# The second mixture's second round: two lists in two quarters each, in place of four lists in one quarter each

## The chip, the cores and the metric

The kernel runs on one core of one Trainium2 chip. The time is the device time of one execution in microseconds (us); three executions of the kernel before gave 761.75, 761.96 and 762.65 us, median 761.96 us.

## The reference

Three layers run one after the other on 2304 tokens of width 512, in float32: windowed attention, a dense feed-forward layer, and a mixture of eight experts of which each token uses the one with the highest logit. The change is in the mixture:

```python
expert_idx = np.argmax(logits, axis=1)
gate_w = probs[np.arange(N), expert_idx]
for e in range(E):                       # E = 8 experts, D = 512, F = 1024
    mask = expert_idx == e
    h = np.maximum(x[mask] @ w1[e], 0.0)      # [n, 512] @ [512, 1024]
    out[mask] = gate_w[mask, None] * (h @ w2[e])   # [n, 1024] @ [1024, 512]
```

How many tokens an expert gets is known only when the logits are there.

## The kernel before, in words

The kernel picks the expert that most tokens chose and computes it for all 17 tiles of 128 tokens; rows of other experts' tokens are not written out. This dense expert is the loop over `e_up` and `e_down`: 40 slots (5 blocks of 4, 4, 4, 3 and 2 tiles, 8 slots each). In slot q TensorE does `e_up(q)`, 12 matmuls into `eh` over 512, 384 or 256 columns by the size of the block, and `e_down(q - 2)`, three matmuls of 512 columns into `eo` for each tile. Both read operands that were split into a high and a low part.

The tokens of the other seven experts are put in lists of 32 rows, one expert to a list. Four lists make a step (class `Quad`): their 128 rows are gathered into one tile `yg`, transposed (`qt`, into `yTh`), multiplied with w1 in two halves of 512 columns, relu'd into `hb`, transposed again into `hTh` and multiplied with w2. All lists have different weights, so list i uses the 32 columns of the array that write rows 32i to 32i+31 of `qo` (line 1227): four matmuls of 32 rows x 512 columns stand one after the other, in plain float32, and each leaves two records in the trace. Such a step has 16 substeps of four matmuls; each substep takes four pieces of weights of 256 KB, in pairs in eight buffers `rw` of 512 KB.

Nothing is scheduled: the order of each engine is the order in which the code is written (`manual_schedule`). `second()` puts extra work behind slots of the dense expert as hooks. Two rounds are put there, `quads[0]` and `quads[1]`: substeps n and n+1 (counted over both rounds) are computed behind slot 15 + 3n/4 and their loads are issued from SP's queue three slots earlier. SP waits there in order until TensorE has read the buffers. The loads of the second round carry a condition (is there such a list?); a list that isn't there is issued and moves nothing. Lists beyond the eight of the two rounds are done behind a branch at the end (line 1476), which is taken when the number of lists is over 8.

Behind the last substep `put` scales the 128 rows with their gates on VectorE (line 1167) and writes them to their tokens' places with an indirect DMA from GpSimd's queue (line 1168).

Of the kernel before, what the change touches and what calls it, by code (L numbers as in the profile page):

```python
# [9 lines left out]
F32 = mybir.dt.float32  # L10
F32R = mybir.dt.float32r
BF16 = mybir.dt.bfloat16
U32 = mybir.dt.uint32
I32 = mybir.dt.int32
AF = mybir.ActivationFunctionType
ALU = mybir.AluOpType
# [7 lines left out]
    trans=[10.354, 10.896, 16.524, 22.659], pglob=[9.223, 14.082, 14.125, 22.293],  # L24
# [12 lines left out]
def kernel(  # L37
# [16 lines left out]
    nc = tc.nc  # L54
    B, H, S, D = q_l.shape
    G = q_g.shape[2]
    P = 128
    DM = H * D
# [4 lines left out]
    KD = DM // P  # L63
    KF = DFF // P
    KF2 = F2 // P
    NTOK = B * S + B * G
    NTILE = B * NT + 1
    QW = 32
    NQ4 = P // QW
    NSTEP = -(-(NTOK // QW + E) // NQ4)  # L70
# [16 lines left out]
        out=tri_bf, in_=ones_bf, pattern=[[1, P]], compare_op=ALU.is_gt, fill=0.0, base=0, channel_multiplier=-1  # L87
# [3 lines left out]
    bigs = const.tile([P, NSTEP], F32, name="bigs")  # L91
    nc.gpsimd.iota(
        bigs, pattern=[[P, NSTEP]], base=2 * NTOK, channel_multiplier=1, allow_small_or_imprecise_dtypes=True
# [22 lines left out]
    NC = 8  # L116
# [9 lines left out]
    ps = at_st.enter_context(tc.tile_pool(name="ps", bufs=3, space=PSUM))  # L126
# [10 lines left out]
    for c in range(2):  # L137
        rows = mask[c * HP : (c + 1) * HP]
        nc.gpsimd.affine_select(
            out=rows[:, :, :HP], in_=rows[:, :, :HP], pattern=[[0, 3], [1, HP]], compare_op=ALU.is_ge, fill=NEG,  # L140
# [184 lines left out]
    class Unit:  # L325
        def __init__(self, n):
            self.b, self.g = divmod(n, 2)
            self.kw = [None, None]
            self.qT = [None, None]
            self.sm = {}  # L330
            self.sg = {}
            self.pn = {}
            self.xs = {}
            self.st = {}
            self.pt = {}
            self.ptA = {}
# [188 lines left out]
    def trans(n, k):  # L525
        u = units[n]
        hl, uu = divmod(k, 2)
        pn = u.pn.pop(k)
        ta = ps.tile([P, 4, P], F32, name="ta", tag="T")
        tb = ps.tile([P, 512], F32, name="tb", tag="T")  # L530
        ptA = get_ptA(n, k)
        ptB = ap_.tile([P, P], F32, name="ptB", tag="ptB")
        u.pt[k] = ptA, ptB
        for i in range(4):
            nc.tensor.transpose(ta[:, i, :], pn[:, i, :], ident)  # L535
        nc.tensor.transpose(tb[:, :P], u.sg.pop(k).rearrange("p i g -> p (i g)"), ident)
        copy(AT["e_ta"], ptA[:, :, G:], ta)
        copy(AT["e_tb"], ptB, tb[:, :P])
# [385 lines left out]

    NS1 = 2
    R = {}

    def pick():  # L930
# [75 lines left out]
    def norms(t0, t1):  # L1006
        sl = slice(t0, t1)
        nc.gpsimd.tensor_tensor(
            out=gt[:, 0, sl], in0=ssq[:, sl], in1=half.to_broadcast([P, t1 - t0]), op=ALU.pow
        )  # L1010
# [117 lines left out]
    outs = dram_disjoint_views(out, NTILE + NSTEP)  # L1128
    w1r = w1.rearrange("e (k p) f -> e k p f", p=P)
    w2r = w2.rearrange("e (k i p) d -> e k p i d", p=P, i=2)  # L1130
    raws = [None] * NC
# [32 lines left out]
    def put(j, ops):  # L1164
        ids = R["ids"]
        ob = rp.tile([P, DM], F32, name="ob", tag="ob0")
        nc.vector.tensor_scalar(out=ob, in0=ops, scalar1=R["gsl"][:, j : j + 1], scalar2=None, op0=ALU.mult)
        nc.gpsimd.indirect_dma_start(
            out=outs[NTILE + j], out_offset=bass.IndirectOffsetOnAxis(ap=ids[:, j : j + 1], axis=0), in_=ob, in_offset=None,
            bounds_check=NTOK - 1, oob_is_err=False,  # L1170
        )
# [4 lines left out]
    class Quad:  # L1176
# [7 lines left out]
        def regs(self, i0, i1):  # L1184
            exi = R["exi"]
            for i in range(i0, i1):
                q = NQ4 * self.j + i
                ev = nc.sync.value_load(exi[0:1, 0, q : q + 1], min_val=0, max_val=E - 1)
                ch = nc.sync.value_load(exi[0:1, 1, q : q + 1], min_val=0, max_val=1) if self.j else None
                self.e.append((ev, {"cond": ch} if self.j else {}))  # L1190
# [15 lines left out]
        def load(self, s):  # L1206
            n = NSUB * self.j + s
            for p in range(2):
                t = self.raw[s, p] = raws[(2 * n + p) % NC].rearrange("p (i d) -> p i d", i=2)
                for i in range(2):  # L1210
                    ev, kw = self.e[2 * p + i]
                    if s < 2 * KD:
                        f, k = divmod(s, KD)
                        src = w1r[bass.ds(ev, 1), k, :, f * 512 : (f + 1) * 512]
                    else:
                        src = w2q[bass.ds(ev, 1), s - 2 * KD]
                    nc.sync.dma_start(out=t[:, i, :], in_=src.rearrange("e p f -> (e p) f"), **kw)

        def mm(self, s):
            first, last = (s % KD == 0, s % KD == KD - 1) if s < 2 * KD else (s == 2 * KD, s == NSUB - 1)  # L1220
            if first:
                self.o = ps.tile([P, 512], F32, name="qo", tag="T")
            a, c = (self.yT, s % KD) if s < 2 * KD else (self.hT, s - 2 * KD)
            ws = [self.raw.pop((s, p)) for p in range(2)]
            for i in range(NQ4):
                cs = slice(QW * i, QW * (i + 1))
                nc.tensor.matmul(self.o[cs], lhsT=a[:, c, cs], rhs=ws[i // 2][:, i % 2, :], start=first, stop=last)
            if last and s < 2 * KD:
                self.hb = rp.tile([P, 512], F32, name="hb")
                nc.scalar.activation(out=self.hb, in_=self.o, func=AF.Relu)  # L1230

        def htr(self, f):
            self.tr(self.hb, self.hT[:, 4 * f : 4 * f + 4, :])
# [2 lines left out]
            put(self.j, self.o)  # L1236


    NES = NEB * KF2
    eb = [Blk() for _ in range(NEB)]  # L1240
    eq = {}
# [70 lines left out]
    def hook(q, *fs):  # L1312
        hooks.setdefault(q, []).extend(fs)

    def second():

        for c in range(6, NC):
            hook(c - 6, lambda c=c: es_split(c))
        for b in range(1, NEB):
            q, nt = KF2 * (b - 1), eblocks[b][1]  # L1320
            if b > 1:
                hook(q + 1, lambda b=b: e_load(b, 0), lambda b=b: e_load(b, 1))
                q += 3
            for i in range(nt):
                hook(q + i, lambda b=b, i=i: e_tr(b, i))
                if i + 2 < nt:
                    hook(q + i, lambda b=b, i=i: e_load(b, i + 2))
        TE = blocks[NB - 2][0] // P
        hook(-11, lambda: norms(0, TE))
        hook(-7, lambda: gates(0, TE))  # L1330
        hook(-5, lambda: members(0, TE))
        hook(8, steps_e)
        hook(9, steps_e2, lambda: members(TE, NTILE), steps1b)
        hook(10, steps1c, lambda: quads[0].regs(0, NQ4))
        hook(11, steps2, lambda: norms(TE, NTILE))
        quads = [Quad(j) for j in range(NS1)]
        hook(12, quads[0].gather)
        hook(13, lambda: gates(TE, NTILE))
        hook(14, quads[0].trans)
        hook(14, lambda: R.update(rl=digits(R["ohhi"], NTILE, NSTEP, gb)))  # L1340
        hook(15, lambda: R.update(gsl=gate_list(R["rl"])))
        hook(26, lambda: R.update(nst=nc.values_load(R["exi"][0:1, 0, NQ:], min_val=0, max_val=NQ)))
        for n in range(0, NS1 * NSUB, 2):
            (j, s), q = divmod(n, NSUB), 15 + 3 * n // 4
            r = quads[j]
            hook(q - 3, lambda r=r, s=s: (r.load(s), r.load(s + 1)))
            hook(q, lambda r=r, s=s: (r.mm(s), r.mm(s + 1)))
            if s in (KD, 2 * KD):
                hook(q, lambda r=r, s=s: r.htr(s // KD - 1))
            if s == KD and j + 1 < NS1:  # L1350
                hook(q, lambda j=j: quads[j + 1].regs(0, NQ4))
            if s == 2 * KD and j + 1 < NS1:
                hook(q, lambda j=j: quads[j + 1].gather())
            if s == NSUB - 4 and j + 1 < NS1:
                hook(q, lambda j=j: quads[j + 1].trans())
            if s == NSUB - 2:
                hook(q, lambda r=r: r.put())

    cvq = [(i, h) for i in range(ncv) for h in range(2)]
    rp = None  # L1360
# [6 lines left out]
    with tc.manual_schedule():  # L1367
# [105 lines left out]
        for i in range(eblocks[NEB - 1][1]):  # L1473
            e_down(NES - 2, [i])
            e_down(NES - 1, [i])
    with tc.If(R["nst"] > NS1 * NQ4):  # L1476
        with tc.manual_schedule():
            for j in range(NS1, NSTEP):
                r = Quad(j)
                r.regs(0, NQ4)  # L1480
                r.gather()
                r.trans()
                for s in range(3):
                    r.load(s)
                for s in range(NSUB):
                    if s + 3 < NSUB:
                        r.load(s + 3)
                    r.mm(s)
                    if s in (KD - 1, 2 * KD - 1):
                        r.htr(s // KD)  # L1490
                r.put()
# [30 lines left out]
```

## Time and profile before

| | |
|---|---|
| device time, three executions | 761.75 / 761.96 / 762.65 us |
| the profiled execution | 760.9 us |
| its span, first to last instruction | 759.2 us |
| TensorE busy | 735.9 us, 97% |
| VectorE, ScalarE, GpSimd busy | 483.2, 371.8, 139.6 us |
| granted TensorE clock, mean | 0.996 |
| HBM read, written | 78.20 MB, 12.08 MB |

The profile is of one execution, so durations in it add up to its own 760.9 us and not to the median. A busy TensorE is one with a matmul in flight; matmuls overlap, so the distance from one start to the next, and not a record's duration, is what a matmul costs in a row. In the timeline a row stands for several records of one kind where it ends in x4 or x16.

### The profile page before, as it was taken

The page shows a single profiled execution, that of the slowest core. Times are in us where ns is not written, and L with a number is a line of the kernel's source. Part 1 is how long each engine was busy: PE and PEld are TensorE (multiplying, and loading weights), DVE is VectorE, ACT ScalarE, POOL GpSimd, SP SyncE. Part 2 cuts the span into 40 slices and gives each one's busy share as a digit, 9 for nine tenths or more (in the row PEclk, how much of TensorE's full clock was granted, in tenths as well). Part 3 has the DMA queues.
Part 4 walks back from the last instruction along what each step waited for, and adds up shares of the span by engine and source line. Part 5 has one row for each costly group of instructions (what it writes and reads, how often), then busy time and mean ns, then how long its engine had stood idle before and what let it go on. Part 6 is the DMA issues. An engine that isn't in the chain of part 4 may idle for free.

```text
span 759.2 us, 14336 instructions
## 1 busy us (share of the span) xinstructions
PE 735.9 (97%) x4989; PEld 590.4 (78%) x4989; DVE 483.2 (64%) x1472; ACT 371.8 (49%) x930; POOL 139.6 (18%) x301
## 2 busy tenths in 40 slices
PE   6999988999999999999999999999999999999996
PEld 5777666788888888888888888888888866677764
DVE  4799988378887757777689867785887411112111
ACT  4899998554555565455565555564212211111110
POOL 3777776312111100000000100000003002011011
PEclk9999999999999999999999999999999999999999
DMA  7587875323333612000200032123101768565440
GB/s 185 132 229 187 228 207 127 106 85 112 112 113 109 213 66 69 1 1 0 98 2 1 0 125 68 45 70 104 51 0 70 244 203 295 182 198 188 133 161 25
DMA packets 70445, 86.22 MB, mean 114 GB/s; under 512 B 27376, under 2 KB 42736, under 8 KB 70368
## 3 DMA queue, kind: packets, MB, share of 16 engines
q1 hardware_dynamic: 63104, 77.39, 34.3%
q0 software_dynamic: 1680, 4.98, 1.7%
q10 hardware_dynamic: 5584, 2.88, 1.3%
q8 instruction: 41, 0.67, 0.4%
q14 instruction: 36, 0.29, 0.1%
HBM read 78.20 MB, written 12.08 MB: 119 GB/s over the span
## 4 chain that ended last, share of the span: by engine, by line
PE 69%; issue 18%; DMA 4%; POOL 3%; DVE 2%; ACT 2%; POOLq 0%; SPq 0%; ACTq 0%
PE yp L865 25%; PE hps L816 25%; PE eh L1271 4%; PE eo L1293 4%; DMA out<-ob,ide 3%; PE pv L563 3%; PE s L467 2%; PE ta L535 2%; PE pv L576 2%; ACT sm L489 1%; POOL pn L511 1%; POOL out L1305 1%; PE pq L395 1%; PE sg L408 1%; DMA q<-in_q_l 1%
## 5 line engine op out<-in xcount | busy, mean ns | idle before, releaser
L816 PE MATMUL hps<-xh,winh 128*128 128x512 f32 (+2 forms) x320 | 115.1, 360 | 1.5 <-DVE g__2977 L832 1.5
L816 PE MATMUL hps<-xl,winh 128*128 128x512 f32 (+2 forms) x320 | 114.4, 358 | 0.0
L816 PE MATMUL hps<-xh,winl 128*128 128x512 f32 (+2 forms) x320 | 114.3, 357 | 0.0
L865 PE MATMUL yp<-woh,gh 128*128 128x512 f32 x272 | 107.4, 395 | 0.0
L865 PE MATMUL yp<-wol,gh 128*128 128x512 f32 x272 | 106.3, 391 | 0.0
L1277 DVE SCALAR_TENSOR_TENSOR el<-eh,eg 128x512 fp32r<-128x512 f32 (+2 forms) x40 | 24.4, 610 | 109.0 <-ACT eg L1276 105.5
L1276 ACT ACTIVATE eg<-eh 128x512 fp32r<-128x512 f32 (+2 forms) x40 | 21.4, 534 | 103.9 <-PE eh L1271 92.8
L816 PEld LDWEIGHTS hps<-xh,winh 128*128 128x128 f32 x320 | 60.3, 188 | 10.6 <-DVE g__2977 L832 1.7
L1305 POOL DMA_INDIRECT out<-ob,ide x17 | 17.1, 1005 | 276.3 <-DVE ob L1302 272.6
L816 PEld LDWEIGHTS hps<-xh,winl 128*128 128x128 f32 x320 | 60.3, 188 | 8.5
L816 PEld LDWEIGHTS hps<-xl,winh 128*128 128x128 f32 x320 | 60.3, 188 | 7.6
L1271 PE MATMUL eh<-exh,wh 128*128 128x512 f32 (+2 forms) x160 | 59.7, 373 | 0.0
L865 PEld LDWEIGHTS yp<-woh,gh 128*128 128x128 f32 x272 | 51.1, 188 | 9.5
L865 PEld LDWEIGHTS yp<-wol,gh 128*128 128x128 f32 x272 | 51.1, 188 | 9.4
L489 ACT ACTIVATE sm<-sm,st 128x160 f32<-128x160 f32 x128 | 53.4, 426 | 9.7 <-DVE st L479 9.6
L1271 PE MATMUL eh<-exh,wl 128*128 128x512 f32 (+2 forms) x160 | 57.3, 358 | 0.8 <-PEq L1476 0.8
L1271 PE MATMUL eh<-exl,wh 128*128 128x512 f32 (+2 forms) x160 | 57.3, 358 | 0.0
L1293 PE MATMUL eo<-wh,eg 128*128 128x512 f32 x136 | 53.3, 392 | 0.0
L1293 PE MATMUL eo<-wl,eg 128*128 128x512 f32 x136 | 53.2, 391 | 0.0
L1293 PE MATMUL eo<-wh,el 128*128 128x512 f32 x136 | 53.1, 391 | 0.0
L511 POOL TENSOR_SCALAR pn<-sm,st 128x128 f32<-128x128 f32 x128 | 48.0, 394 | 14.8 <-DVE st L507 8.6
L849 DVE TENSOR_TENSOR wol<-wof,woh 128x512 fp32r<-128x512 f32 x64 | 43.9, 686 | 0.0
(799 smaller groups left out, 1594.8 us busy)
## 6 DMA issues: line engine op xcount, KB each, us to landing
rw<-in_moe_w SPq DMA_DIRECT2D x128, 256.0 KB
raw<-in_moe_w_out SPq DMA_DIRECT2D x12, 512.0 KB
raw<-in_moe_w_in SPq DMA_DIRECT2D x11, 512.0 KB
k<-in_k_l SPq DMA_DIRECT2D x16, 256.0 KB
ysc<-y SPq DMA_DIRECT2D x16, 256.0 KB
rw<-in_moe_w SPq DMA_DIRECT2D x8, 512.0 KB
ye<-ysc SPq DMA_DIRECT2D x16, 256.0 KB
q<-in_q_l SPq DMA_DIRECT2D x15, 256.0 KB
```

Of the source, the lines that this page charges most:

```text
L467: nc.tensor.matmul(sj[j][c * HP : (c + 1) * HP, tt, :], lhsT=u.qT[hl][j * D : (j + 1) * D, q0 : q0 + HP], rhs=u.kw[hl][j * D : (j + 1) * D ...
L489: nc.scalar.activation(out=sm[:, i, :], in_=sm[:, i, :], func=AF.Exp, scale=-1.0, bias=st[:, 0, i : i + 1], accum_out=st[:, 1, i : i + 1],)
L511: eng_of[AT["f4"][i]].tensor_scalar(out=pn[:, i, :].rearrange("p (c x) -> p c x", c=2), in0=sel(sm[:, i, :]), scalar1=st[:, 2, i : i + 1], ...
L563: nc.tensor.matmul(pv[j * D : (j + 1) * D, tt, c0:c1], lhsT=v[:, 2 * hl + j, t, :], rhs=ptA[:, 2 * tt + j, c0:c1], start=tt == 0 and c0 == ...
L816: nc.tensor.matmul(hp_[:, :n], lhsT=wt[:, kk, fs], rhs=xt, start=kk == 0 and i == 0, stop=kk == KD - 1 and i == 2)
L849: nc.vector.tensor_tensor(out=wol, in0=wof[f // 2][:, f % 2, :], in1=woh.bitcast(F32), op=ALU.subtract)
L865: nc.tensor.matmul(B_.yp[i], lhsT=gt[:, cs], rhs=wt, start=f == 0 and k == 0, stop=f == KF - 1 and k == 2)
L1271: nc.tensor.matmul(hps[:, :n], lhsT=w[:, fs], rhs=x, start=kk == 0 and i == 0, stop=kk == KD - 1 and i == 2)
L1276: nc.scalar.activation(out=gh, in_=hps[:, :n], func=AF.Relu)
L1277: nc.vector.scalar_tensor_tensor(out=gl, in0=hps[:, :n], scalar=0.0, in1=gh.bitcast(F32), op0=ALU.max, op1=ALU.subtract)
L1293: nc.tensor.matmul(B_.yp[i], lhsT=a[:, cs], rhs=w, start=f == 0 and k == 0, stop=f == KF2 - 1 and k == 2)
L1305: nc.gpsimd.indirect_dma_start(out=outs[t], out_offset=bass.IndirectOffsetOnAxis(ap=ide[:, t : t + 1], axis=0), in_=ob, in_offset=None, bo ...
```

## The change

The first round stays a `Quad`, with its hooks two slots apart in place of one and a half. The second round becomes a new class `Half`, for two lists. Each list has two of the array's column quarters: quarter 2x + l is list l with columns from half x of its weights. In the up product both halves of w1's columns are made at once, 4 substeps of 4 matmuls over 512 columns in place of 8 such substeps; in the down product each half makes 256 of the 512 output columns, 8 pieces of 4 matmuls over 256 columns in place of 8 over 512. The weights of a list come in 8 pieces of 512 KB in place of 16 of 256 KB. `put` joins the halves: one scaled copy on VectorE, one copy on ScalarE between partitions, one more scaling on VectorE, and a write of 64 rows. Lists 7 and 8, which the second round held, now go behind the branch as another `Half`, and the branch is taken when there are more than 6 lists.

```diff
+    class Half(Quad):
...
+        def load(self, s):
+            for l in range(2):
+                t = self.raw[s, l] = raws[(2 * (NSUB + s) + l) % NC]
+                ev, kw = self.e[l]
+                if s < KD:
+                    src, dst = w1r[bass.ds(ev, 1), s].rearrange("e p f -> (e p) f"), t
+                else:
+                    src = w2r[bass.ds(ev, 1), s - KD].rearrange("e p i d -> (e p) i d")
+                    dst = t.rearrange("p (i d) -> p i d", i=2)
+                nc.sync.dma_start(out=dst, in_=src, **kw)
+
+        def mm(self, s):
+            if s % KD == 0:
+                self.o = ps.tile([P, 512], F32, name="qo", tag="T")
+            ws = [self.raw.pop((s, l)) for l in range(2)]
+            n = DM if s < KD else DM // 2
+            for c in (s,) if s < KD else (2 * (s - KD), 2 * (s - KD) + 1):
+                for i in range(NQ4):
+                    x, l = divmod(i, 2)
+                    if s < KD:
+                        a, w0 = self.yT[:, c, self.r0 + l * QW :][:, :QW], x * DM
+                    else:
+                        f, k = divmod(c, KF2 // 2)
+                        a, w0 = self.hT[:, k, (2 * f + l) * QW :][:, :QW], (c % 2) * DM + x * n
+                    nc.tensor.matmul(
+                        self.o[i * QW : (i + 1) * QW, :n], lhsT=a, rhs=ws[l][:, w0 : w0 + n],
+                        start=c == 0, stop=c == (KD if s < KD else KF2) - 1,
+                    )
+            if s == KD - 1:
+                self.hb = rp.tile([P, 512], F32, name="hb")
+                nc.scalar.activation(out=self.hb, in_=self.o, func=AF.Relu)
...
+        def put(self):
...
+            nc.vector.tensor_scalar(out=ob[rr, same], in0=self.o[rr, :n], scalar1=g, scalar2=None, op0=ALU.mult)
+            nc.scalar.copy(out=ob[rr, other], in_=self.o[o0 : o0 + 2 * QW, :n])
+            nc.vector.tensor_scalar(out=ob[rr, other], in0=ob[rr, other], scalar1=g, scalar2=None, op0=ALU.mult)
...
+        quad, half2 = Quad(0), Half(1, 0)
...
-        for n in range(0, NS1 * NSUB, 2):
-            (j, s), q = divmod(n, NSUB), 15 + 3 * n // 4
-            r = quads[j]
+        for n in range(0, NSUB + 2 * KD, 2):
+            r, s, q = (quad, n, 15 + n) if n < NSUB else (half2, n - NSUB, 15 + n)
             hook(q - 3, lambda r=r, s=s: (r.load(s), r.load(s + 1)))
             hook(q, lambda r=r, s=s: (r.mm(s), r.mm(s + 1)))
...
+            if r is quad:
+                if s in (KD, 2 * KD):
+                    hook(q, lambda s=s: quad.htr(s // KD - 1))
+                if s == KD:
+                    hook(q, half2.regs)
+                if s == 2 * KD:
+                    hook(q, half2.gather)
+                if s == NSUB - 2:
+                    hook(q, quad.put)
+                    hook(q + 1, half2.trans)
+            elif s == KD - 2:
+                hook(q + 1, half2.htr)
+            elif s == 2 * KD - 2:
+                hook(q, half2.put)
...
-    with tc.If(R["nst"] > NS1 * NQ4):
+    with tc.If(R["nst"] > NQ4 + 2):
         with tc.manual_schedule():
-            for j in range(NS1, NSTEP):
+            r = Half(1, 2 * QW)
...
+            r.put()
+            for j in range(2, NSTEP):
```

On TensorE, the last hook of the second round, behind slot 37, in the kernel before; `rw4` to `rw7` are weight buffers, x2 is two quarters of the array:

```order
L1293 MATMUL eo1_8597<-wh5_6676,el_8634 128x512
L1227 MATMUL qo_8556<-rw4_6349,hTh_8132 32x512 x2
L1227 MATMUL qo_8556<-rw5_6468,hTh_8132 32x512 x2
L1227 MATMUL qo_8556<-rw6_6584,hTh_8132 32x512 x2
L1227 MATMUL qo_8556<-rw7_6674,hTh_8132 32x512 x2
L1271 MATMUL eh_8710<-exh_8287,wh0_6129 128x256
```

The same hook in the changed kernel; between the lines of `rw4` and `rw5`, and of `rw6` and `rw7`, these two alternate, four of each:

```order
L1365 MATMUL eo1_8476<-wh5_6676,el_8508 128x512
L1276 MATMUL qo_8517<-rw4_6349,hTh_8483 32x256
L1276 MATMUL qo_8517<-rw5_6468,hTh_8483 32x256
...
L1276 MATMUL qo_8517<-rw6_6584,hTh_8483 32x256
L1276 MATMUL qo_8517<-rw7_6674,hTh_8483 32x256
...
L1343 MATMUL eh_8603<-exh_8206,wh0_6129 128x256
```

So this hook has 16 matmuls over 256 columns where it had 8 over 512. There are two such hooks and two of 8 matmuls over 512 columns in the new second round, behind slots 31, 33, 35 and 37; before, the second round had eight hooks of 8 matmuls over 512 columns, behind slots 27, 28, 30, 31, 33, 34, 36 and 37.

On TensorE, the transposes of `hb` in the second round stand alone in the changed kernel, behind slot 34; before, there were two of them, each behind a hook's matmuls:

```order
L1365 MATMUL eo1_8476<-wh4_6586,el_8391 128x512
L1202 MATMUL qt_8484<-ident_63,hb_8456 128x128 x4
L1343 MATMUL eh_8494<-exh_8206,wh0_6129 128x256
L1343 MATMUL eh_8494<-exh_8206,wl0_6130 128x256
L1343 MATMUL eh_8494<-exl_8208,wh0_6129 128x256
```

One of the two transposes is gone, and the one that is left moved out of a hook. The transposes of `yg` for the second round are alone in the same way, behind slot 30.

On VectorE, the end of the program of the changed kernel, from the second part of slot 35 to the branch (`el` is the dense expert's, `ob` the second round's output):

```order
L1349 SCALAR_TENSOR_TENSOR el_8548<-eh_8534,eg_8547 128x256
L1349 SCALAR_TENSOR_TENSOR el_8571<-eh_8557,eg_8570 128x256
L1296 TENSOR_SCALAR ob_8596<-qo_8517,gsl_7604 64x256
L1298 TENSOR_SCALAR ob_8596<-ob_8596,gsl_7604 64x256
L1349 SCALAR_TENSOR_TENSOR el_8617<-eh_8603,eg_8616 128x256
L1551 COMPARE_AND_BRANCH
```

Two narrow scalings stand where one of 128x512 stood, and the second of them waits for ScalarE's copy; the `el` of slot 38 is behind both, as it was behind the one before.

## Rows read from the trace of the kernel before

**Rows 1.** The page, part 2: 40 slices of the span, TensorE busy in tenths.

```profile
PE   6999988999999999999999999999999999999996
```

**Rows 2.** Busy time by stretch: us, busy us (instructions) of each engine, clock, DMA share, GB/s.

```profile
592.00:608.00 16.00, 16.00 (x79) 13.33 (x78) 7.07 (x23) 4.74 (x11) 0.00 (x0) 1.00 0.84 278
610.00:745.00 135.00, 134.98 (x800) 95.02 (x798) 22.54 (x41) 23.50 (x46) 12.88 (x13) 1.00 0.59 190
```

**Rows 3.** Waits of TensorE from 590 to 759: who for whom, us, times, longest.

```profile
PE eh L1271 <- PEq L1476: 0.8, 1, 0.8
```

**Rows 4.** Instructions that write or read qo, same columns, for the second round.

```profile
690.00:745.00 55.00, 15.39 (x128) 3.34 (x128) 0.55 (x1) 1.20 (x2) 1.00 0.42 130
```

**Rows 5.** Timeline, TensorE around one lone hook: start us, us, engine, line, operation.

```profile
660.90 0.39 PE L1293 MATMUL eo<-wh,el 128*128 128x512 f32 x1
661.22 1.92 PE L1227 MATMUL qo<-rw,hTh 128*32 128x512 f32 x16
663.08 0.50 PE L1271 MATMUL eh<-exh,wh 128*128 128x512 f32 x1
663.42 0.40 PE L1271 MATMUL eh<-exh,wl 128*128 128x512 f32 x1
```

**Rows 6.** Timeline, weight loads of the same hook.

```profile
661.22 0.16 PEld L1227 LDWEIGHTS qo<-rw,hTh 128*32 128x32 f32 x8 [0.35 <-issue]
661.68 0.13 PEld L1227 LDWEIGHTS qo<-rw,hTh 128*32 128x32 f32 x4 [0.30 <-issue]
662.11 0.13 PEld L1227 LDWEIGHTS qo<-rw,hTh 128*32 128x32 f32 x4 [0.30 <-issue]
```

**Rows 7.** Timeline, TensorE: a hook with transposes behind it.

```profile
708.55 0.40 PE L1293 MATMUL eo<-wh,el 128*128 128x512 f32 x1
...
710.73 0.66 PE L1203 MATMUL qt<-ident,hb 128*128 128x128 f32 x4
711.14 0.42 PE L1271 MATMUL eh<-exh,wh 128*128 128x384 f32 x1
711.40 0.33 PE L1271 MATMUL eh<-exh,wl 128*128 128x384 f32 x1
```

**Rows 8.** Timeline, TensorE: transposes alone between the large matmuls.

```profile
591.47 0.39 PE L1293 MATMUL eo<-wh,el 128*128 128x512 f32 x1
591.70 0.60 PE L1151 MATMUL tt<-ident,ye 128*128 128x128 f32 x4
...
592.37 0.39 PE L1271 MATMUL eh<-exh,wl 128*128 128x512 f32 x1
```

**Rows 9.** Attention, four tiles at a time: one group in the timeline.

```profile
102.74 0.78 PE L467 MATMUL s<-kw,qT 64*64 64x160 f32 x16
```

**Rows 10.** The same line (467) over the run: duration ns min/median/max, first and last start.

```profile
L467 PE MATMUL s<-kw,qT x512: 296/296/348, 8.3 to 135.9; 64*64 64x160 f32 x171
```

**Rows 11.** DMA from 674.7 to 740: packets, MB, share; then issues with KB each.

```profile
q1 hardware_dynamic: 4944, 8.92, 45.2%
...
rw<-in_moe_w SPq DMA_DIRECT2D x64, 256.0 KB
```

**Rows 12.** Waits of the SP queue from 580 to 759.

```profile
SPq L1217 <- PE qo L1227: 54.6, 25, 9.4
```

**Rows 13.** Timeline, TensorE: the last hook, and the gap at the branch.

```profile
742.06 0.39 PE L1293 MATMUL eo<-wh,el 128*128 128x512 f32 x1
...
744.45 0.28 PE L1271 MATMUL eh<-exh,wl 128*128 128x256 f32 x1
744.57 0.28 PE L1271 MATMUL eh<-exl,wh 128*128 128x256 f32 x1
...
748.92 0.35 PE L1271 MATMUL eh<-exh,wl 128*128 128x256 f32 x1 [0.78 <-PEq L1476]
```

**Rows 14.** Timeline, GpSimd from 744 on (in brackets: idle time before).

```profile
745.47 0.98 POOL L1168 DMA_INDIRECT out<-ob,ids  x1 [17.54 <-DVE ob L1167]
753.57 0.98 POOL L1305 DMA_INDIRECT out<-ob,ide  x1 [7.11 <-DVE ob L1302]
```

More of the change, by code (lines that the diff above doesn't have):

```diff
@@ L923, in pieces_end @@
         ]
-    NS1 = 2
     R = {}
@@ L1236, in put, with __init__, regs, trans @@
             put(self.j, self.o)
+    class Half(Quad):
+        def __init__(self, j, r0):
+            super().__init__(j)
+            self.r0 = r0
+        def regs(self):
+            i0 = self.r0 // QW
+            super().regs(i0, i0 + 2)
+        def trans(self):
+            self.yT = rp.tile([P, KD, P], F32, name="yTh")
+            self.tr(self.y, self.yT)
+        def load(self, s):
[28 more added lines that the diff above has]
+                nc.scalar.activation(out=self.hb, in_=self.o, func=AF.Relu)
+        def htr(self):
+            self.hT = rp.tile([P, KF2, P], F32, name="hTh")
+            self.tr(self.hb, self.hT[:, :4, :])
+        def put(self):
+            j, r0, n = self.j, self.r0, DM // 2
+            rr = slice(r0, r0 + 2 * QW)
+            x = r0 // (2 * QW)
+            same, other = slice(x * n, (x + 1) * n), slice((1 - x) * n, (2 - x) * n)
+            o0 = 2 * QW - r0
+            g = R["gsl"][rr, j : j + 1]
+            ob = rp.tile([P, DM], F32, name="ob", tag="ob0")
+            nc.vector.tensor_scalar(out=ob[rr, same], in0=self.o[rr, :n], scalar1=g, scalar2=None, op0=ALU.mult)
+            nc.scalar.copy(out=ob[rr, other], in_=self.o[o0 : o0 + 2 * QW, :n])
+            nc.vector.tensor_scalar(out=ob[rr, other], in0=ob[rr, other], scalar1=g, scalar2=None, op0=ALU.mult)
+            ids, m = R["ids"][:, j : j + 1], r0 + 2 * QW
+            if r0:
+                ids = rp.tile([P, 1], U32, name="idh")
+                nc.vector.tensor_copy(out=ids, in_=R["ids"][:, j : j + 1])
+                nc.vector.tensor_copy(out=ids[:r0], in_=bigs[:r0, j : j + 1])
+                nc.vector.memset(ob[:r0], 0.0)
+            nc.gpsimd.indirect_dma_start(
+                out=outs[NTILE + j], out_offset=bass.IndirectOffsetOnAxis(ap=ids[:m], axis=0),
+                in_=ob[:m], in_offset=None, bounds_check=NTOK - 1, oob_is_err=False,
+            )
@@ L1333, in second @@
         hook(9, steps_e2, lambda: members(TE, NTILE), steps1b)
-        hook(10, steps1c, lambda: quads[0].regs(0, NQ4))
+        hook(10, steps1c, lambda: quad.regs(0, NQ4))
         hook(11, steps2, lambda: norms(TE, NTILE))
-        quads = [Quad(j) for j in range(NS1)]
-        hook(12, quads[0].gather)
+        hook(12, quad.gather)
         hook(13, lambda: gates(TE, NTILE))
-        hook(14, quads[0].trans)
+        hook(14, quad.trans)
         hook(14, lambda: R.update(rl=digits(R["ohhi"], NTILE, NSTEP, gb)))
@@ L1342, in second @@
         hook(26, lambda: R.update(nst=nc.values_load(R["exi"][0:1, 0, NQ:], min_val=0, max_val=NQ)))
-        for n in range(0, NS1 * NSUB, 2):
-            (j, s), q = divmod(n, NSUB), 15 + 3 * n // 4
-            r = quads[j]
+        for n in range(0, NSUB + 2 * KD, 2):
+            r, s, q = (quad, n, 15 + n) if n < NSUB else (half2, n - NSUB, 15 + n)
             hook(q - 3, lambda r=r, s=s: (r.load(s), r.load(s + 1)))
             hook(q, lambda r=r, s=s: (r.mm(s), r.mm(s + 1)))
[L1348 to L1357, printed above, removed]
+            if r is quad:
[12 more added lines that the diff above has]
+                hook(q, half2.put)
     cvq = [(i, h) for i in range(ncv) for h in range(2)]
@@ L1475 @@
             e_down(NES - 1, [i])
-    with tc.If(R["nst"] > NS1 * NQ4):
+    with tc.If(R["nst"] > NQ4 + 2):
         with tc.manual_schedule():
-            for j in range(NS1, NSTEP):
+            r = Half(1, 2 * QW)
+            r.regs()
+            r.gather()
+            r.trans()
+            for s in range(3):
+                r.load(s)
+            for s in range(2 * KD):
+                if s + 3 < 2 * KD:
+                    r.load(s + 3)
+                r.mm(s)
+                if s == KD - 1:
+                    r.htr()
+            r.put()
+            for j in range(2, NSTEP):
                 r = Quad(j)
```

## The prediction

> **What bounds the kernel now.** I read the page's slices first, then busy time by stretch, then what TensorE waited for. The slices show TensorE at nine tenths or more from about slice 8 to slice 39 [rows 1]; in the stretch of the hooks, 610 to 745, it is busy for all of it at a granted clock of 1.00 (the 2.4 GHz level), while VectorE and ScalarE are busy about a sixth of it [rows 2]. From 590 to the end TensorE waited once, 0.8 us, for its own sequencer at the branch (line 1476) [rows 3]. So what is taken from TensorE's queue between slot 15 and the end comes off the time, unless something else becomes late; what is added there is paid in full. SP's loads are not the bound: SP stood 54.6 us waiting for TensorE to read `qo`'s buffers [rows 12], so the loads are early.
>
> **The change, part by part.** All prices are distances between starts, since durations overlap.
>
> *What a hook costs now.* Around a lone hook the last `eo` starts at 660.90, the second `eh` at 663.42 [rows 5]. Without the hook, two steps of 0.23 (591.47 to 591.70, [rows 8]) would lie between them. The hook costs 2.52 - 0.46 = 2.06 us. The last hook, before columns of 256: 742.06 to 744.45 is 2.39, less 0.23 and 0.12 (744.45 to 744.57), is 2.04 [rows 13]. I take 2.05.
>
> *What it consists of.* A hook has 8 matmuls, 16 records. The weight loads come in bunches of four: eight at 661.22 (two bunches at once), four at 661.68, four at 662.11, each bunch done in 0.13 to 0.16 [rows 6]. So four quarters run together, and a hook is four rounds of four records: the third begins 0.43 after the second. Four rounds are 1.72, and 0.33 is paid at the edges. Within a round the four weight loads are over in a third of the time, so the 512 columns set the pace and not the loads.
>
> *Removed.* The second round has 128 records [rows 4], that is eight hooks: 8 x 2.05 = 16.4 us. Two transposes of `hb` stood behind hooks: 708.55 to 711.40 is 2.85, less 0.23, less 0.17 (an `eh` of 384 columns, three quarters of 0.23), is 2.45, so 0.40 beyond the hook [rows 7]; twice 0.40. The transposes of `yg` stood behind a hook of the first round, 0.40 more. Together 17.6 us.
>
> *Added.* Four hooks. Two are the up product: 8 matmuls over 512 columns as before, 2.05 each. Two are the down product: 16 matmuls over 256 columns, eight rounds instead of four. If a round's time goes with its columns, 8 x 0.215 = 1.72 and the hook again costs 2.05. The transposes of `yg` and of `hb` now stand alone; alone such a group costs 591.47 to 592.37, 0.90 less twice 0.23, 0.44 [rows 8]. Together 4 x 2.05 + 2 x 0.44 = 9.1 us.
>
> *The narrow rounds, from both sides.* Before, no round of 256 columns and four quarters is in the trace. The nearest is attention: 16 records of 160 columns, four tiles together, take 0.78 us from first start to last end [rows 9]. A single record lasts 0.30 (296 ns, [rows 10]); that leaves 0.48 for three distances between rounds, 0.16 each, the first weight loads included; 0.43 x 160/512 would be 0.134. So rounds do shrink with their columns and keep at most 0.026 each. With that, eight rounds cost 0.2 more per hook, 0.4 in all. The other end is that a round costs 0.43 whatever its columns: two hooks then cost 1.72 more each, 3.4 in all. Less than proportion is excluded: the columns still have to pass at the rate of the 512. I take proportion, since attention's row lies close to it.
>
> The Trainium skill (TensorE: Matmul & The Clock Gate, "Wait — 56ns, not 53.3ns?") speaks against narrow matmuls: with hardware decoding off, about 62 ns go to each matmul, which binds once the array's work is shorter; four records in 0.215 us are 54 ns each. Counted per record, 32 of them are 1.98 us a hook by that rule, 0.26 more, 0.5 us in all. Attention's row disagrees: 12 records in 0.48 us are 40 ns each.
>
> *First round.* Same matmuls, same eight hooks, two slots apart instead of one and a half: the sum is unchanged.
>
> *Loads.* A hook of the new second round reads 2.1 MB, as a hook of the first does. It can start when its four of the eight buffers `rw` have been read, which is at the end of the hook before the previous one; four slots and one hook lie between. In the narrowest block a slot is 12 x 0.12 + 6 x 0.23 = 2.8 us, so the load has 4 x 2.8 + 2.05 = 13.3 us. At the 278 GB/s of 592 to 608 [rows 2] it takes 7.6 us. TensorE would wait only below 160 GB/s. SP issues 16 loads for this round in place of 64 and reads four list entries fewer. Cost nothing; if the cover is gone, each late load adds what it is late.
>
> *The end.* `put` becomes three short steps in a row on VectorE, ScalarE and VectorE. GpSimd started its write at 745.47 and was idle 7.11 us before its next one at 753.57 [rows 14]; a start even 1.5 us later is hidden. `el` of slot 38 is behind both scalings, but its reader is two slots away. The dense expert's last slots and the writes behind them stay. The branch's 0.8 us of idle TensorE stays; it stands four matmuls later in the program, which may move it by 0.2 either way.
>
> *Sum.* -17.6 + 9.1 = -8.5 us. The profiled execution took 760.9 (span 759.2 and 1.7 around it), so 752.4 with a span of about 750.7. The median of the three executions is 1.06 above the profiled one; carried over, 753.5 us.
>
> **Rivals.**
>
> A. *The narrow rounds don't shrink.* A 256-column round takes 0.43. Then the down hooks cost 3.77 each and 5.1 us are left: 756.9. For it: no such round is in the trace. Against it: attention's 0.16 for 160 columns.
>
> B. *TensorE begins to wait for loads or hand-offs.* The second round's hooks now stand two narrow slots apart, 5.6 us and the hook, 7.7 us for 2.1 MB; were this to go on, it would need 273 GB/s, about what 592 to 608 shows. But only three such sets follow one another, and SP waits already. If the last two sets were each 2 to 3 us late: 757.5 to 759.5.
>
> C. *Slower: the branch is taken.* Place: the end, where lists 7 and on are done with nothing beside them. The point from which it decides: a seventh list. Its price: the branch holds 19 steps; 18 full ones with 8 hooks' matmuls each (16.4 us), 295 us of TensorE alone, so above 1050 us. Against it: from 674.7 on the SP queue moved 8.92 MB, dense tiles included, for 64 issued pieces of the second round [rows 11]. A list's weights are 16 pieces of 256 KB, 4.2 MB: two lists are 8.4 MB, three would be 12.6. So there are four and two, six lists, and six is not over six.
>
> D. *No change.* The end is set by something beside TensorE. Against it: [rows 2, 3].
>
> **How the numbers follow.** Forecast 0.82, A 0.08, B 0.05, C 0.02, D 0.03. The forecast's own spread: 0.5 us of scatter, 0.4 for narrow rounds, 0.2 for the branch, and the 1.06 between profiled run and median, which may not carry over: 752.3 to 754.5. The range goes up to A, since A's end is an unknown cost's bound: 752.0 to 757.0; B's upper part, C and D are left out. 0.2%, 1.5 us, is about what a measurement of this kernel can tell from no change: faster 0.95, same 0.03, slower 0.02.
>
> **What would show it.** In the profile after: TensorE busy from slot 15 to the branch with no wait for a DMA; the second round's 128 records of `qo` over 512 columns replaced by 32 over 512 and 64 over 256, the latter in two hooks of about 1.9 us (A: about 3.6); SP still waiting for `qo`; 16 loads of 512 KB; nothing from the body of the branch. The prediction is wrong if TensorE waits for `rw`, if a down hook takes over 2.5 us, or if the end of the last `eo` lies less than 7.5 us earlier.

## The result and the profile after

The changed kernel took 756.03, 751.50, 751.49, 751.39 and 751.73 us, median 751.50 us, beside 761.96 us; the ratio is 0.9873 (95% interval 0.9841 to 0.9905). Forecast were 753.5 us and a range of 752.0 to 757.0, so the forecast time is 2.0 us too long and the median lies 0.5 us below the range.

The profiled execution of the changed kernel is the one of 756.03 us, 3.6 us longer than the 752.4 forecast for it. First the page: span, busy time, and TensorE in 40 slices.

```profile
span 754.2 us, 14060 instructions
PE 729.5 (97%) x4953; PEld 589.8 (78%) x4953; DVE 483.6 (64%) x1473; ACT 371.4 (49%) x929; POOL 140.2 (19%) x301
PE   8799998999999999999999999999999999999996
HBM read 69.81 MB, written 11.94 MB: 108 GB/s over the span
```

The slices look as in [rows 1], with 6.4 us less of TensorE work. The line of HBM is 8.39 MB lower, but that is no saving: it equals 32 loads of 256 KB, as many as the kernel before issued for the two lists that aren't there. The loads' DMA queue moved as many MB as before (packets, MB, share; before, then after):

```profile
q1 hardware_dynamic: 63104, 77.39, 34.3%
```

```profile
q1 hardware_dynamic: 61824, 77.38, 34.3%
```

The stretch of the hooks, in the columns of [rows 2], is again filled by TensorE at a granted clock of 1.00:

```profile
610.00:740.00 130.00, 129.98 (x781) 97.09 (x780) 23.60 (x44) 23.31 (x46) 12.90 (x13) 1.00 0.60 199
```

So TensorE's queue still sets the pace there, and the difference must be in its length. The tiles that TensorE writes for the dense expert mark that queue's two ends: count, duration in ns (min, median, max), first and last start. Before, then after:

```profile
L1271 PE MATMUL eh<-exh,wh x160: 278/389/504, 517.0 to 749.2; 128*128 128x512 f32 x96, 128*128 128x384 f32 x32, 128*128 128x256 f32 x32
L1293 PE MATMUL eo<-wh,el x136: 388/389/399, 532.3 to 753.5; 128*128 128x512 f32 x136
```

```profile
L1343 PE MATMUL eh<-exh,wh x160: 277/389/504, 520.2 to 742.8; 128*128 128x512 f32 x96, 128*128 128x384 f32 x32, 128*128 128x256 f32 x32
L1365 PE MATMUL eo<-wh,el x136: 388/389/398, 535.5 to 748.5; 128*128 128x512 f32 x136
```

From the first `eh` to the last `eo` it was 753.5 - 517.0 = 236.5 us and is 748.5 - 520.2 = 228.3: 8.2 us less (8.23 from the single records), beside 8.5 forecast. But the mixture began 3.2 us later, and that lies in code that the change doesn't touch. The first feed-forward matmul in the attention stage, before and after:

```profile
141.00 0.48 PE L816 MATMUL hps<-xh,winh 128*128 128x512 f32 x1
```

```profile
144.27 0.47 PE L816 MATMUL hps<-xh,winh 128*128 128x512 f32 x1
```

In that stage TensorE waited for a DMA of the attention's values, 0.6 us in all before, and after:

```profile
PE pv L563 <- DMA vb<-va: 3.1, 3, 2.2
```

The same changed kernel, profiled again below, has this wait at 0.6 us and starts that matmul at 141.02. So the 3.3 us are scatter between executions of an unchanged stage, and no cost of the change.

The hooks, in TensorE's timeline of the changed kernel: an up hook, the lone transposes of `hb`, a down hook, and the gap at the branch:

```profile
711.77 0.40 PE L1365 MATMUL eo<-wh,el 128*128 128x512 f32 x1
712.10 1.92 PE L1276 MATMUL qo<-rw,yTh 128*32 128x512 f32 x16
713.96 0.38 PE L1343 MATMUL eh<-exh,wh 128*128 128x256 f32 x1
714.18 0.28 PE L1343 MATMUL eh<-exh,wl 128*128 128x256 f32 x1
...
725.71 0.39 PE L1365 MATMUL eo<-wh,el 128*128 128x512 f32 x1
725.94 0.60 PE L1202 MATMUL qt<-ident,hb 128*128 128x128 f32 x4
...
726.49 0.28 PE L1343 MATMUL eh<-exh,wl 128*128 128x256 f32 x1
...
728.96 0.39 PE L1365 MATMUL eo<-wh,el 128*128 128x512 f32 x1
729.28 1.93 PE L1276 MATMUL qo<-rw,hTh 128*32 128x256 f32 x32
731.14 0.39 PE L1343 MATMUL eh<-exh,wh 128*128 128x256 f32 x1
731.36 0.28 PE L1343 MATMUL eh<-exh,wl 128*128 128x256 f32 x1
...
742.94 0.28 PE L1343 MATMUL eh<-exh,wl 128*128 128x256 f32 x1
744.42 0.36 PE L1343 MATMUL eh<-exl,wh 128*128 128x256 f32 x1 [1.19 <-PEq L1551]
```

From the last `eo` to the second `eh`, less 0.23 and 0.12 as in [rows 13]: the up hook costs 2.41 - 0.35 = 2.06 us and the down hook 2.40 - 0.35 = 2.05. The lone transposes, in the same way, cost 0.78 - 0.35 = 0.43. Sixteen records of 512 columns take 1.92 and 32 of 256 columns take 1.93: a round's time goes with its columns. What [rows 4] counted as 128 records is now

```profile
L1276 PE MATMUL qo<-rw,hTh x64: 379/379/403, 729.3 to 738.5; 128*32 128x256 f32 x64
L1276 PE MATMUL qo<-rw,yTh x32: 592/592/617, 712.1 to 722.5; 128*32 128x512 f32 x32
```

TensorE's only wait from 580 to the end answers to [rows 3]; it grew from 0.8 to 1.2 us:

```profile
PE eh L1343 <- PEq L1551: 1.2, 1, 1.2
```

SP still waits for `qo` (65.8 us in three lines in place of the 54.6 us of [rows 12], from 580 on), so the loads are still early:

```profile
SPq L1216 <- PE qo L1226: 36.8, 9, 8.5
SPq L1261 <- PE qo L1276: 14.8, 4, 8.2
SPq L1261 <- PE qo L1226: 14.2, 4, 8.3
```

`put` starts on VectorE at 739.00 and its third step ends at 740.26; GpSimd's write follows, and the idle time before its next one is the 7.11 us of [rows 14] again:

```profile
740.53 0.93 POOL L1305 DMA_INDIRECT out<-ob,ids  x1 [16.00 <-DVE ob L1298]
748.57 0.99 POOL L1377 DMA_INDIRECT out<-ob,ide  x1 [7.11 <-DVE ob L1374]
```

### The profile page after: what moved, and what is told of

Same layout as the page of the kernel before. It is cut to its first block, busy times and chain, and to the rows that moved or that the text cites. A ratio compares the mean times of both kernels' runs of the same rounds, so it can differ in the third digit from the quotient of the medians.

```text
span 754.2 us, 14060 instructions
## 1 busy us (share of the span) xinstructions
PE 729.5 (97%) x4953; PEld 589.8 (78%) x4953; DVE 483.6 (64%) x1473; ACT 371.4 (49%) x929; POOL 140.2 (19%) x301
## 3 DMA queue, kind: packets, MB, share of 16 engines
q1 hardware_dynamic: 61824, 77.38, 34.3%
## 4 chain that ended last, share of the span: by engine, by line
PE 75%; issue 13%; DMA 4%; POOL 4%; DVE 2%; ACT 2%; SPq 1%; POOLq 0%; ACTq 0%
PE yp L865 25%; PE hps L816 25%; PE eh L1343 7%; PE eo L1365 6%; DMA out<-ob,ide 3%; PE pv L563 2%; PE s L467 2%; PE pv L576 2%; PE ta L535 1%; POOL pn L511 1%; DMA vb<-va 1%; PE pq L395 1%; POOL out L1377 1%; PE sg L408 1%; PE tt L1150 1%
## 5 line engine op out<-in xcount | busy, mean ns | idle before, releaser
L816 PEld LDWEIGHTS hps<-xh,winh 128*128 128x128 f32 x320 | 60.3, 188 | 10.6 <-DVE g__2977 L832 1.7
```

Of the source, the lines that this page charges most:

```text
L816: nc.tensor.matmul(hp_[:, :n], lhsT=wt[:, kk, fs], rhs=xt, start=kk == 0 and i == 0, stop=kk == KD - 1 and i == 2)
```

## The experiments

Theory: the time follows the length of TensorE's queue in the mixture, and that length is a sum of hooks (columns and a fixed edge for each visit). Rivals: narrow rounds cost something of their own; the new places of the hooks matter; the loads are near to being late; the difference is scatter. Each run's profile gives the stretch from the first `eh` to the last `eo`, and in it the one gap at the branch, as TensorE's idle time. Other than the two rows named "profiled first", the runs come from three chips, and each ratio is to executions of the kernel before on the same chip, with medians of 761.02 us (both kernels again, no second round, hooks of a whole group), 761.58 (one slot apart, loads late) and 760.96 (the others):

| kernel | median us (lowest to highest) | ratio to before (95%) | stretch us | gap at the branch us | stretch less gap us |
|---|---|---|---|---|---|
| before, profiled first | 761.96 (761.75 to 762.65) | | 236.48 | 0.8 | 235.7 |
| before, again | 760.82 (759.27 to 763.19) | 0.9997 (0.9983 to 1.0011) | 236.87 | 1.1 | 235.8 |
| changed, profiled first | 751.50 (751.39 to 756.03) | 0.9873 (0.9841 to 0.9905) | 228.25 | 1.2 | 227.1 |
| changed, again | 752.25 (751.25 to 753.07) | 0.9876 (0.9855 to 0.9897) | 228.51 | 1.3 | 227.2 |
| no second round | 743.02 (742.34 to 743.67) | 0.9762 (0.9741 to 0.9782) | 218.41 | 0.4 | 218.0 |
| hooks of a whole group | 750.64 (750.32 to 751.54) | 0.9865 (0.9840 to 0.9889) | 226.91 | 1.9 | 225.0 |
| whole groups, last at 37 | 750.38 (749.05 to 751.03) | 0.9856 (0.9837 to 0.9874) | 225.71 | 0.7 | 225.0 |
| places of before | 751.89 (750.68 to 752.68) | 0.9880 (0.9860 to 0.9900) | 227.68 | 0.4 | 227.3 |
| rounds of 128 columns | 752.90 (751.04 to 755.65) | 0.9900 (0.9868 to 0.9931) | 227.91 | 0.8 | 227.1 |
| one slot apart | 753.12 (752.83 to 753.60) | 0.9897 (0.9881 to 0.9914) | 229.09 | 1.3 | 227.8 |
| one slot apart, loads late | 753.22 (751.63 to 755.39) | 0.9893 (0.9864 to 0.9923) | 228.95 | 1.0 | 228.0 |

**The two kernels again,** without an edit, in five rounds each.

> The kernel before, unchanged, against itself on one chip. If the 2 us by which the changed kernel's timed runs were faster than the sum (751.5 against 753.5) is scatter of the attention stage from one execution to the next, the copies differ here by up to 2 us too and the profile's attention stage ends at another time than 144.98 us (last pv start). If it belongs to the program, the copies agree within 0.5 us.

> The changed kernel, unchanged. My theory (a second round of four hooks at 2.05 us in place of eight): 8.0 to 8.7 us below the kernel before from the first qo to the end of the last eo, whatever the attention stage does; in total 8 to 11 us below. The rival that the gain depends on the execution: less than 6 us below in some of the rounds.

Measured: the kernel before 760.82 us over 12 executions, and 761.02 over the 17 beside them, which ran from 759.08 to 763.59; the changed kernel 752.25 us, 8.8 us less. The two medians of the kernel before agree to 0.2 us while its single executions differ by over 4, and its last `pv` start is 146.87 us in this profile in place of 144.98. So 761.96 was a high draw, and part of the first difference of 10.5 us is scatter. The gain of 8 to 11 us (0.9855 to 0.9897 of 761) is not: the slowest of the five executions of the changed kernel, 753.07, is 6.0 us below the fastest of the 17, so the rival of less than 6 us falls. From the first `qo` to the end of the last `eo` the two profiles differ by 8.4 us (143.74 to 135.35), within the 8.0 to 8.7 expected.

**No second round.** The loop ends behind the first round, and the second round's gather, transposes, products and `put` are left out: the lists 5 and 6 are not computed.

```diff
-        for n in range(0, NSUB + 2 * KD, 2):
+        for n in range(0, NSUB, 2):
...
-                if s == KD:
-                    hook(q, half2.regs)
-                if s == 2 * KD:
-                    hook(q, half2.gather)
...
-                    hook(q + 1, half2.trans)
```

> The changed kernel with the second round left out (lists 5 and 6 are not computed and their rows not written). By the sum this takes away 4 hooks of 2.05 and two lone groups of transposes of 0.44, so 9.1 us below the changed kernel, and TensorE's distance from the first qo to the last eo shrinks by 9.1. If the second round were partly hidden (it waited for loads, or filled time that TensorE would idle anyway), it is clearly less than 9.

Measured: 743.02 us, 9.2 less than the changed kernel of the same rounds; stretch less gap 9.2 less. The stretch itself is 10.1 less, since the gap at the branch also went from 1.3 to 0.4. The forecast's price for what was added, 9.1 us, holds in TensorE's queue: nothing of it is hidden behind other work.

**Rounds of 128 columns.** The down product's matmuls are cut in two once more, so a down hook is 64 records.

```diff
-                for i in range(NQ4):
+                for i, m0 in [(i, m0) for m0 in ((0,) if s < KD else (0, n // 2)) for i in range(NQ4)]:
...
+                    m1 = m0 + (n if s < KD else n // 2)
...
-                        self.o[i * QW : (i + 1) * QW, :n], lhsT=a, rhs=ws[l][:, w0 : w0 + n],
-                        start=c == 0, stop=c == (KD if s < KD else KF2) - 1,
+                        self.o[i * QW : (i + 1) * QW, m0:m1], lhsT=a, rhs=ws[l][:, w0 + m0 : w0 + m1],
+                        start=c == 0 and m0 == 0,
+                        stop=c == (KD if s < KD else KF2) - 1 and m1 == n,
```

> The changed kernel with each down matmul of 256 columns cut into two of 128, so 32 matmuls, 64 records and 16 rounds to a hook. If a round still takes its columns' time (0.107), the down hooks stay at 2.06 us. If the weight loads of a round (0.13 for a bunch of four) set the pace, 16 x 0.13 + 0.33 = 2.4, 0.7 us more in all. If each record costs 62 ns, 64 x 0.062 + 0.33 = 4.3, 4.5 us more in all.

Measured in its timeline:

```profile
725.90 0.39 PE L1367 MATMUL eo<-wh,el 128*128 128x512 f32 x1
726.22 1.95 PE L1277 MATMUL qo<-rw,hTh 128*32 128x128 f32 x64
728.11 0.39 PE L1345 MATMUL eh<-exh,wh 128*128 128x256 f32 x1
728.33 0.28 PE L1345 MATMUL eh<-exh,wl 128*128 128x256 f32 x1
```

2.43 - 0.35 = 2.08 us a hook, 0.02 to 0.03 more than with half as many records; 2.4 (the pace of the weight loads) and 4.3 (62 ns a record) are excluded. Less the 0.33 of edges, 1.75 us for 64 records is 27 ns each, 55 ns for each of the 32 matmuls.

The Trainium skill (TensorE: Matmul & The Clock Gate, "Wait — 56ns, not 53.3ns?") states about 62 ns for each matmul with hardware decoding off. An estimate by that figure is 2.0 us for the 32 matmuls, or 4.0 if each record pays it; the measured 1.75 is below both, with four quarters at work together. No run here shows how decoding was set, so it is shown that this price isn't paid in this kernel, and not that the figure is wrong.

**Hooks of a whole group.** Six hooks of four substeps, at slots 15, 19, 23, 27, 32 and 38, in place of twelve of two.

```diff
...
+        HQ = (15, 19, 23, 27, 32, 38)
+        for m, q in enumerate(HQ):
+            r, g = (quad, m) if m < 4 else (half2, m - 4)
+            ss = range(KD * g, KD * g + KD)
+            hook(HQ[m - 1] if m else 12, lambda r=r, ss=ss: [r.load(s) for s in ss])
...
+            hooks.setdefault(q, []).insert(0, lambda r=r, ss=ss: [r.mm(s) for s in ss])
...
```

> The changed kernel with four substeps to a hook, so 6 hooks (slots 15, 19, 23, 27, 32, 38) in place of 12, each using all eight weight buffers; same matmuls. If the 0.33 us at a hook's edges is paid once per visit, 6 x 0.33 = 2.0 us less, minus 0.1 for two transposes that now stand alone: 1.9 us below the changed kernel. If the edge belongs to the matmuls and not to the visit: the same time. If the loads (4.2 MB, 15 us at 278 GB/s, with no second set of buffers) come late: TensorE waits for rw, and the time is the same or up to 5 us longer.

A second kernel of the same kind has the last hook and its `put` at 37.

```diff
-        HQ = (15, 19, 23, 27, 32, 38)
+        HQ = (15, 19, 23, 27, 32, 37)
...
-        hook(38, half2.put)
+        hook(37, half2.put)
```

> The kernel with whole groups of four substeps, its last hook behind slot 37 in place of 38. The gap at the branch was 2.3 us there, with 7 matmuls queued in place of 17; if put at slot 38 made the branch late, this brings the gap back to about 1.4 and the time is 0.7 us less (some 750.0). If its loads (done 3.4 us before the hook needed them, a slot is 2.8) become late, the gain is lost: the same time or up to 1.5 us more.

Measured: 750.64 and 750.38 us, 1.6 and 1.9 below the changed kernel's 752.25. The last hook of the second one, and its gap at the branch:

```profile
730.38 0.39 PE L1365 MATMUL eo<-wh,el 128*128 128x512 f32 x1
730.70 3.66 PE L1276 MATMUL qo<-rw,hTh 128*32 128x256 f32 x64
734.29 0.39 PE L1343 MATMUL eh<-exh,wh 128*128 128x256 f32 x1
734.51 0.28 PE L1343 MATMUL eh<-exh,wl 128*128 128x256 f32 x1
...
738.40 0.28 PE L1343 MATMUL eh<-exh,wl 128*128 128x256 f32 x1
739.39 0.35 PE L1343 MATMUL eh<-exl,wh 128*128 128x256 f32 x1 [0.71 <-PEq L1550]
```

4.13 - 0.35 = 3.78 us for a hook of twice the size, beside twice 2.05 = 4.10. The 0.33 of edges is paid for each visit and not for each substep, as the split of the 2.05 into 1.72 and 0.33 has it. Six visits fewer are 2.0 us; stretch less gap went down by 2.1 to 2.2 in both. In the kernel with the last hook at 38 the gap at the branch took 0.7 of it back:

```profile
741.65 0.47 PE L1365 MATMUL eo<-wh,eg 128*128 128x512 f32 x1 [1.90 <-PEq L1550]
```

With the last hook at 37 the gap fell from 1.9 to 0.7, and the stretch by the same 1.2 us; from start to start, as the expectation counts, the gap is 2.3 and 1.0. This kernel is the fastest of those that compute everything, 10.6 us below the kernel before, though its 750.38 and the other's 750.64 can't be told apart.

**Places of before.** The first round's hooks go back to the spacing of one and a half slots, the second round's to 27, 28, 30 and 31.

```diff
-            r, s, q = (quad, n, 15 + n) if n < NSUB else (half2, n - NSUB, 15 + n)
+            r, s, q = (quad, n, 15 + 3 * n // 4) if n < NSUB else (half2, n - NSUB, (27, 28, 30, 31)[(n - NSUB) // 2])
```

> The changed kernel with the first round's eight hooks at the old one and a half slots (15 to 25) and the four new ones behind slots 27, 28, 30 and 31. My theory counts only what stands in TensorE's queue, so the same time as the changed kernel within 0.5 us. If the wider spacing is part of the gain (fewer waits, or a better place for put and the branch): 1 us or more above.

Measured: 751.89 us, and stretch less gap as in the changed kernel, 227.3 beside 227.1 and 227.2. In TensorE's work the new places give and cost nothing; its gain is the four hooks fewer and the transposes. The gap at the branch is 0.4 us here and 1.2 to 1.3 with the new places; the medians are too close to show whether that is paid.

**One slot apart.** The second round's hooks stand at 34, 35, 36 and 37.

```diff
-            r, s, q = (quad, n, 15 + n) if n < NSUB else (half2, n - NSUB, 15 + n)
+            r, s, q = (quad, n, 15 + n) if n < NSUB else (half2, n - NSUB, 34 + (n - NSUB) // 2)
...
-                hook(q + 1, half2.htr)
+                hooks.setdefault(q + 1, []).append(half2.htr)
```

> The changed kernel with the second round's four hooks behind slots 34, 35, 36 and 37, one slot apart; same matmuls, same loads. If loads are early only because the hooks stand two slots apart (a set of 2.1 MB takes 7.6 us at 278 GB/s, and its four buffers come free a hook before the previous one), TensorE waits for rw before the third hook for about 1.4 us and before the fourth for 2.7: 4 us above the changed kernel (3 to 6). If the loads have no such limit, or are paced by something else: within 0.7 us of it.

Measured: 753.12 us, 0.9 above the changed kernel's 752.25. TensorE didn't wait for `rw`; its one new wait is for the copy of the transposed `hb`:

```profile
PE qo L1276 <- ACT hTh L1203: 0.7, 1, 0.7
```

But this run doesn't answer the question on the loads. The loads stay three slots ahead, and so those for the third and fourth hook are issued before the first and second hook have read the same buffers. In this kernel the second round's up product is computed with later substeps' weights, and no load had to wait for a hook. So a further run put them where they must wait.

**One slot apart, loads late.** The same four places; the loads for the third and fourth hook stand right behind the first and second, so the cover is one hook and two slots.

```diff
...
+        for m in range(4):
+            q, s = 34 + m, 2 * m
+            if m == 2:
+                hook(q, half2.htr)
+            if m < 2:
+                hook(31 + m, lambda s=s: (half2.load(s), half2.load(s + 1)))
+            hook(q, lambda s=s: (half2.mm(s), half2.mm(s + 1)))
+            if m < 2:
+                hook(q, lambda s=s: (half2.load(s + 4), half2.load(s + 5)))
+        hook(37, half2.put)
```

> The second round's four hooks stand at slots 34, 35, 36 and 37 instead of 31, 33, 35 and 37, and the loads for the third and the fourth hook are issued right behind the first and the second hook, so that each load has one hook and two slots' steps of cover. Nothing of the computation is left out. Theory (the forecast's cover of the loads, by which TensorE waits only for what a load is late): between the end of one hook and the start of the next but one there are 2.05 + 2 x 2.8 = 7.65 us; 2.1 MB take 7.6 us at 278 GB/s, plus about 2 us from issue to landing of a first piece, so TensorE waits 1 to 3 us for rw before the third hook and again 0 to 3 us before the fourth, and 0.7 us for the copy of hTh that now stands one slot behind the transposes' source: 754 to 757.5 us beside 752 of the changed kernel. Rival (the loads run at a higher rate when nothing else is queued, so that even this cover is enough): no wait for rw, at most the 0.7 us for hTh, 751.5 to 753.

Measured: 753.22 us. All of TensorE's waits from 640 on:

```profile
PE eh L1343 <- PEq L1556: 1.0, 1, 1.0
PE qo L1276 <- ACT hTh L1203: 0.7, 1, 0.7
```

There is no wait for `rw`, as the rival has it, and the step from 278 GB/s to a wait falls; the median lies 0.2 us above the rival's 753. The DMA view of 712 to 740 in 40 slices of 0.7 us shows why; below it are the times from issue to landing of the second round's 16 loads, and the start of the fourth hook:

```profile
GB/s 0 0 23 0 0 0 290 53 354 53 316 73 143 313 398 404 313 392 404 386 348 310 348 375 369 401 389 386 199 82 6 0 0 0 0 0 0 47 9 0
DMA to landing us min/median/max: 3.7/5.9/8.1
...
733.63 0.64 PE L1276 MATMUL qo<-rw,hTh 128*32 128x256 f32 x8
```

In the 15 slices from 721.1 to 731.6 most of the last eight pieces came, at 310 to 404 GB/s. Their 4.19 MB moved from 720.1 to 733.2, 320 GB/s in the mean, and the fourth hook began 0.5 us behind; at 278 they would have ended at 735.2, 1.5 us late. So this cover is just enough. The 278 GB/s of 592 to 608 [rows 2] is a mean and not what the queue can give: in 40 slices, the first 1.2 us of that stretch have no transfer, and others go up to 410 GB/s.

## Why the prediction was right, and where its sizes were off

**The bound.** Right. Stretch less gap falls by 8.6 us (235.7 to 227.1; again 235.8 to 227.2), and every kernel of the table stands where a sum of hooks puts it, within 0.3 us: one round less, six visits less, or 0.7 us for the one wait. Of the prediction's signs of being wrong, one shows by its letter in the first profile: the last `eo` starts 5.0 us earlier (753.5 to 748.5) and not 7.5. That sign counts from the start of the program and so takes in the 3.3 us of the attention stage; in the changed kernel's second profile the last `eo` starts at 745.4, 8.1 us earlier.

**Hook, up and down.** Right: 2.06 and 2.05 us for the 2.05 taken. The lone transposes cost 0.43, beside 0.44 taken. The 0.43 us of a round stands in [rows 6] between the third and the fourth bunch (661.68 to 662.11), and not between the second and the third.

**Narrow rounds.** Proportion was right. The 0.4 us kept for them from attention's row wasn't needed: 0.01 us at 256 columns (1.93 beside 1.92), and at 128 columns a hook is 0.03 longer. Rival A, 3.77 a hook, is excluded. Attention's row speaks against the 62 ns by records only: its 12 records are six matmuls, 80 ns each.

**Loads.** No wait, as forecast, and with more room than worked out: the rate taken, 278 GB/s, is a mean over a stretch that has idle slices in it. Rival B was given 0.05; the run with late loads shows that hooks one slot apart in place of two still get their weights in time, with half a us to spare.

**The end.** `put`'s three steps are hidden, as forecast. The gap at the branch is a term that was mis-sized: 0.8, "may move it by 0.2", and it came out as 1.2 and 1.3; the kernel before itself has 0.8 and 1.1. It is what makes the first two profiles differ by 8.23 and not by 8.6. Over all kernels it lies between 0.4 and 1.9 us. What sets it was not settled: moving the last group by one slot took it from 1.9 to 0.7. The two kernels with 0.4 have it 22 and 31 us ahead of the last `eo`, the others 1 to 5 us.

**Rivals C and D.** Behind the gap at the branch stand only rows of the dense expert, and all 96 records of the second round's `qo` lie ahead of it, so the branch wasn't taken, and four and two lists is right. C's price was one step too high: the tokens are 4 x (512 + 32) = 2176, the 17 tiles, and not 2304, so the branch holds 18 steps, 17 of them full. D fell with the stretch.

**From the profiled execution to the median.** Here the time went off. The sum for an execution like the profiled one was 752.4; with 3.3 us of attention, 0.4 of the gap and 8.6 in place of 8.5 it is 756.0, and the profiled one took 756.03. To the 752.4, 1.06 us were added since the median of three lay above the profiled one. The 17 further executions of the kernel before have their median at 761.02, near the profiled 760.9, so there was little to add: without it the forecast is within 0.2 us of the changed kernel's second median, 752.25, which is closer than the scatter and so in part luck. The other 0.75 us to 751.50 lies within the scatter of that kernel's executions. The forecast's own spread, 0.5 us of scatter, was too small: the attention stage alone moved by 3.3 us between two executions of one kernel.

## What to carry to other kernels

Where one engine's queue is full, price an edit as the distance between the unchanged instructions on either side of it, once for each visit and once for its work, and add up only what stays in that queue. Look for column quarters that work for lists that aren't there: two lists in two quarters each halve the hooks, and narrow rounds cost hardly more than their columns, here down to 128. Merge visits where the buffers allow it, and don't carry the offset of a three-run median over to a forecast of a tenth of a per cent.

## What the runs showed that was not expected

- 64 records of 128 columns on four column quarters run at 27 ns each, weight loads included and edges left out; no price for each matmul is to be seen (0.03 us for 32 more records in a hook).
- The edge of a visit of float32 column-quarter matmuls between 128*128 ones is 0.33 to 0.34 us, whether the visit has 16, 32 or 64 records (hooks of 2.06, 2.05 and 3.78 us, less 1.72, 1.72 and 3.44 for the columns).
- The page's HBM line was 8.39 MB higher before, as much as the 32 loads that moved nothing would have read; the DMA queue's own line doesn't have them (77.39 and 77.38 MB).
- One kernel's attention stage can end 3.3 us later in one execution than in another, with 2.5 us more of TensorE waiting for one DMA (3.1 beside 0.6).
- TensorE's gap at an untaken branch lies between 0.4 and 1.9 us in eleven profiles; two profiles of one kernel agree within 0.4 us.
